# A first batch worked by halves of its heads, w_in begun on half of its depth, and other PSUM banks and more of the squares on GpSimd for the first product

## The chip, the cores and the metric

The kernel runs on one core of one Trainium2 chip. The metric is device time in microseconds (us) of that core; lower is better. Before the change the median was 289.12 us over four runs (288.58 to 289.61), so single runs differ by about 0.3%. All times below that begin with a point on a time axis ("at 31.12") are microseconds from the start of one traced execution; a trace is one execution.

A ratio is the mean time of one kernel's fast runs over the mean of the other's fast runs of the same rounds, so it is not quite the ratio of the medians that are quoted beside it.

## The reference

An attention without a score matrix feeds a layer with a sine-based activation:

```
q_s = softmax(q) over the 64 columns of a head
k_s = softmax(k) over the 576 positions
kv  = k_s^T v                    (64 x 64 per head)
x   = q_s kv                     -> 4608 tokens x 512
h   = x @ w_in                   (512 x 2048)
g   = h + sin(alpha * h)^2 / alpha
out = g @ w_out                  (2048 x 512)
```

There are 8 batches of 576 positions and 8 heads. The tokens are worked in 9 tiles of 512 (t = 0 to 8), so tile 1 needs batch 1 of the attention.

## The kernel before

TensorE (PE) multiplies, ScalarE (ACT) takes exponentials, sines, some squares and copies, VectorE (DVE) normalises and adds, GpSimd (POOL) takes the other squares and issues the loads of w_in, of w_out and of some of v of batch 0, SyncE (SP) issues nearly all the rest. The start loads batch 0 and builds x transposed in four slices `xT[:, 0..3]`, each 128 deep; slices 0 and 1 need one half of the heads (`ii = 0`), slices 2 and 3 the other.

```python
load("q", q, 0, halves=True); load("k", k, 0, halves=True)     # SP's queue, halves of the heads
...
GP_CP(held, staged["q", 0][...])                  # holds POOL's queue until half of q is there
... v in three pieces on POOL's queue ...
for c0, c1 in ((0, 256), (256, 512), (512, 1024), (1024, 1536), (1536, 2048)):
    load_win(c0, c1)                              # two DMAs each, cast to bf16 on the way
...
for ii in range(2):
    kv_mm(0, ii, ps_e, split=True)
    kv_norm(0, ii, ii + 1)
for c in range(4):
    xp = ps_h.tile([128, MF], F32, name="hp", tag="h")
    attn_chunk(0, c, 0, 8, xp)
    (ACT_CP, DVE_CP)[c % 2](xT[:, c, 0:MF], xp)
nc.scalar.activation(zero, zero, AX.Sin)          # loads the sine table
```

The first tile of tokens is then 16 blocks of 128 columns of w_in. Each is four matmuls into a PSUM buffer, a sine, a square on the engine that a letter names (D, P or A), and a sum on DVE, which frees the buffer. Blocks use four buffers of `ps_h` in turn, and two more of `ps_e` where `wide` says so. The product with w_out takes the four `ps_h` buffers for its accumulators.

```python
def mm_h(t, ni, wide=None, k0=0, k1=4):
    ...
    elif wide and ni % 6 in ((2, 3) if t == 0 else (4, 5)):
        hp = wide()
    else:
        hp = ps_h.tile([128, MF], F32, name="hp", tag="h")
...
for ni in range(nN):
    h_slot(0, ni, "DPAPPAPPAPPAPPAP"[ni], lag, lent)
    flush(lag, 1)                                 # sum of block ni - 1
    if ni in late:
        late[ni]()                                # q and k of batch 1, rest of w_out
...
os = o_quad(0, accs, [DVE_CP, ACT_CP, DVE_CP, ACT_CP])   # 64 matmuls with w_out
take(os, 20)
... small attention product: the last 64 positions of batch 0 ...
take(os, 26)
... batch 1: exp, normalise, transpose ...
take(os, 8)
kv_mm(1, 0, ps_e, split=True)                     # needs v of batch 1
```

The softmax here doesn't subtract the row's maximum and nothing guards it: scores larger than these inputs give would overflow.

## Time and profile before

| | before |
|---|---|
| time, median | 289.12 us |
| traced span | 286.8 us |
| PE busy | 274.9 us (96%) |
| first product with w_in | 15.74 us |
| first sine / first square on POOL | 17.73 / 19.06 us |
| small attention product | 34.09 us |
| first cast of v of batch 1 | 41.35 us |
| first product of tile 1 | 47.23 us |

The last rows are starting times in the trace.

```profile
15.74 1.95 PE L234 MATMUL hp<-xT,win 128*128 128x512 bf16 x8
...
41.35 1.17 ACT L131 CAST vb<-st_v 128x1152 bf16<-128x1152 f32 x1 [0.20 <-DMA st_v<-in_v_dram]
...
47.23 2.97 PE L234 MATMUL hp<-xT,win 128*128 128x512 bf16 x13
```

The traced execution took 288.60 us, as little as the fastest of the four timed ones (288.58) and 0.5 us less than their median. A difference between this trace and another one is not yet a difference between two kernels.

### The profile page before, as it was taken

The page shows a single profiled execution, that of the slowest core. Times are in us where ns is not written, and L with a number is a line of the kernel's source. Part 1 is how long each engine was busy: PE and PEld are TensorE (multiplying, and loading weights), DVE is VectorE, ACT ScalarE, POOL GpSimd, SP SyncE. Part 2 cuts the span into 40 slices and gives each one's busy share as a digit, 9 for nine tenths or more (in the row PEclk, how much of TensorE's full clock was granted, in tenths as well). Part 3 has the DMA queues.
Part 4 walks back from the last instruction along what each step waited for, and adds up shares of the span by engine and source line. Part 5 has one row for each costly group of instructions (what it writes and reads, how often), then busy time and mean ns, then how long its engine had stood idle before and what let it go on. Part 6 is the DMA issues. An engine that isn't in the chain of part 4 may idle for free.

```text
span 286.8 us, 4259 instructions
## 1 busy us (share of the span) xinstructions
PE 274.9 (96%) x1570; PEld 130.6 (46%) x1570; DVE 188.5 (66%) x281; ACT 226.6 (79%) x320; POOL 81.6 (28%) x77
## 2 busy tenths in 40 slices
PE   1899999999999999999999999999999999999994
PEld 0444454445454445444544454445444444444443
DVE  3867775899968668756775677757674555555412
ACT  4889756999489999899889988998877777777500
POOL 4859420674766571005300530032000000000000
PEclk9999999999999999999999999999999999999999
DMA  7999999946799957129910990116011111111142
GB/s 253 309 205 242 269 391 408 307 169 191 167 199 402 361 184 120 38 43 358 289 37 21 336 308 27 37 39 139 17 39 37 37 37 39 37 37 38 41 109 73
DMA packets 37381, 45.77 MB, mean 160 GB/s; under 512 B 15968, under 2 KB 20848, under 8 KB 37360
## 3 DMA queue, kind: packets, MB, share of 16 engines
q1 hardware_dynamic: 32032, 39.98, 46.3%
q0 software_dynamic: 5136, 5.38, 10.2%
q8 instruction: 12, 0.20, 0.3%
q10 hardware_dynamic: 192, 0.14, 0.2%
q14 instruction: 9, 0.07, 0.1%
HBM read 36.71 MB, written 9.44 MB: 161 GB/s over the span
## 4 chain that ended last, share of the span: by engine, by line
PE 84%; DMA 7%; DVE 5%; POOL 1%; ACT 1%; issue 1%; SPq 0%; POOLq 0%
PE hp L234 38%; PE op L254 35%; DMA st_v<-in_v_dram 4%; PE hh L234 3%; PE kvp L157 2%; PE xp L206 2%; DMA qT<-qn 2%; DMA st_q<-in_q_dram 1%; DVE qs L144 1%; PE op L532 1%; PE op L234 1%; ACT s L240 1%; DVE qn L146 1%; POOL qn L146 1%; POOL s L244 1%
## 5 line engine op out<-in xcount | busy, mean ns | idle before, releaser
L250 DVE SCALAR_TENSOR_TENSOR g<-s,inva_sb,hp 128x512 bf16<-128x512 f32 x130 | 96.1, 745 | 64.1 <-ACT s L242 54.2
L234 PE MATMUL hp<-xT,win 128*128 128x512 bf16 x520 | 129.7, 379 | 0.0
L254 PE MATMUL op<-wout,g 128*128 128x512 bf16 x496 | 124.2, 379 | 0.0
L240 ACT ACTIVATE s<-hp,alpha_sb 128x512 f32<-128x512 f32 x130 | 87.6, 682 | 25.4 <-PE hp L234 24.3
L234 PEld LDWEIGHTS <-win 128*128 128x128 bf16 x576 | 56.3, 98 | 67.4 <-issue 0.4
L254 PEld LDWEIGHTS <-g 128*128 128x128 bf16 x560 | 54.1, 98 | 61.7 <-issue 0.9
L242 ACT ACTIVATE s<-s 128x512 f32<-128x512 f32 x112 | 70.5, 630 | 3.5
L146 POOL TENSOR_TENSOR qn<-qe,qs 128x1152 bf16<-128x1152 bf16 x12 | 25.3, 2128 | 73.2 <-DVE qs L140 63.1
L244 POOL TENSOR_TENSOR s<-s 128x512 f32<-128x512 f32 x29 | 30.5, 1061 | 24.8 <-ACT s L240 24.3
L260 DVE COPY o<-op 128x512 f32<-128x512 f32 (+2 forms) x33 | 22.1, 669 | 9.6 <-PE op L254 7.1
L117 ACT ACTIVATE ke<-st_k 128x1152 bf16<-128x1152 f32 x16 | 17.9, 1151 | 4.8 <-DMA st_k<-in_k_dram 4.1
L117 ACT ACTIVATE qe<-st_q 128x1152 bf16<-128x1152 f32 x16 | 17.9, 1156 | 2.8 <-DMA st_q<-in_q_dram 2.8
L139 DVE TENSOR_REDUCE qs<-qe 128x36 f32<-128x2304 bf16 x5 | 12.8, 2553 | 8.7 <-ACT qe L117 8.6
L131 POOL CAST vb<-st_v 128x1152 bf16<-128x1152 f32 x12 | 13.6, 1162 | 10.4 <-DMA st_v<-in_v_dram 10.4
L254 PE MATMUL hp<-wout,g 128*128 128x512 bf16 x64 | 15.1, 379 | 0.0
L209 DVE CAST xT<-xp 128x512 bf16<-128x512 f32 (+1 forms) x18 | 13.4, 742 | 0.0
L117 ACT ACT_TABLE_LOAD x7 | 9.0, 1283 | 1.3 <-PEq L546 1.2
L157 PEld LDWEIGHTS <-ke 64*128 64x128 bf16 x288 | 8.2, 93 | 3.5 <-ACT s L242 1.3
L157 PE MATMUL kvp<-vb,ke 64*128 64x130 bf16 x288 | 9.7, 216 | 0.0
L234 PE MATMUL hh<-xT,win 128*128 128x512 bf16 x40 | 9.4, 379 | 0.0
L144 DVE TENSOR_REDUCE qs<-qe 128x18 f32<-128x1152 bf16 x6 | 8.0, 1329 | 2.1 <-ACT qe L117 2.1
L206 PE MATMUL xp<-qT,kbd 128*128 128x256 bf16 (+1 forms) x40 | 8.2, 286 | 0.4 <-DVE xT L209 0.3
(68 smaller groups left out, 117.9 us busy)
## 6 DMA issues: line engine op xcount, KB each, us to landing
out_dram<-o SPq DMA_DIRECT2D x70, 128.0 KB, 2.3
st_q<-in_q_dram SPq DMA_DIRECT2D x6, 1152.0 KB, 6.3
st_k<-in_k_dram SPq DMA_DIRECT2D x6, 1152.0 KB, 8.2
st_v<-in_v_dram SPq DMA_DIRECT2D x6, 1152.0 KB, 10.3
st_q<-in_q_dram SPq DMA_DIRECT2D x4, 576.0 KB, 5.5
st_k<-in_k_dram SPq DMA_DIRECT2D x4, 576.0 KB, 7.1
wout<-in_moe_w_out_dram POOLq DMA_DIRECT2D x4, 512.0 KB, 11.2
win<-in_moe_w_in_dram POOLq DMA_DIRECT2D x6, 256.0 KB, 7.1
```

The costliest lines, as they stand in the source:

```text
L117: nc.scalar.activation(dst[:, :, ii * 128:(ii + 1) * 128].rearrange("p j (x d) -> p x j d", x=2), src[:, ii::2], AX.Exp)
L131: engs[ii](vv[:, 2 * ii:2 * ii + 2, :, 0:D], staged["v", b][:, ii::2])
L146: engs[ii % len(engs)].tensor_tensor(qn[:, ii].rearrange("p j (x d) -> p j x d", x=2), qe[:, ii], part.unsqueeze(3).to_broadcast([128, J, ...
L157: nc.tensor.matmul(kvp[:, e, ii * 130:(ii + 1) * 130], ke[r, j, ii * 128:(ii + 1) * 128], vt[r, j, ii * 130:(ii + 1) * 130], start=(j == 0 ...
L206: nc.tensor.matmul(xp[:, e, 0:n], kt[:, e, ii], qT[:, ii, j0:j1, e * 64:(e + 1) * 64], start=True, stop=True)
L234: nc.tensor.matmul(hp, win[:, ki, ni * 128:(ni + 1) * 128], xT[:, ki, t * MF:(t + 1) * MF], start=(ki == 0), stop=(ki == 3))
L240: nc.scalar.activation(s, hp, AX.Sin, scale=alpha_sb[:, ni:ni + 1])
L242: nc.scalar.activation(s, s, AX.Square)
L244: nc.gpsimd.tensor_tensor(s, s, s, op=ALU.mult)
L250: nc.vector.scalar_tensor_tensor(G[t][:, ni], in0=s, scalar=inva_sb[:, ni:ni + 1], in1=hp, op0=ALU.mult, op1=ALU.add)
L254: nc.tensor.matmul(acc, G[t][:, ni, j * 128:(j + 1) * 128], wout[:, ni, :], start=(ni == 0), stop=(ni == nN - 1))
L260: eng(o[:, cols], acc)
```

## The change

The intent is that PE starts on w_in earlier. Batch 0 is worked by halves: q, k and v of the first half of the heads are loaded and used before k and v of the second half. When slices 0 and 1 of xT are there, four blocks of w_in do their first slices, while the other half is still worked on. These four blocks need four `ps_h` buffers, so the extra buffers of `ps_e` go to blocks 4, 5, 9, 10, 14, 15. The row of squares gives POOL 12 in place of 10. Two transposes of q move from the start into the w_out product.

```diff
-    for c0, c1 in ((0, 256), (256, 512), (512, 1024), (1024, 1536), (1536, 2048)):
-        load_win(c0, c1)
+    GP_CP(singles.tile([128, 1], F32, name="held"), staged["k", 0][:, 0, 0, 0:1])
+    load0(GP, "v", v, 1, 0, 5)
+    load0(GP, "v", v, 1, 5, 9)
+    load_win(0, 512, slice(0, 2))
+    load_win(0, 512, slice(2, 4))
+    for c0 in (512, 1024, 1536):
+        load_win(c0, c0 + 512)
 ... cut: exp, cast, transposes and kv of the first half, warm-up matmuls ...
+    nc.scalar.activation(zero, zero, AX.Sin)
+    xp = [ps_h.tile([128, MF], F32, name="hp", tag="h") for _ in range(2)]
+    for c in range(2):
+        attn_chunk(0, c, 0, 8, xp[c])
+    DVE_CP(xT[:, 0, 0:MF], xp[0])
+    ACT_CP(A["qT", 0][:, 1, 0:8], tp1)
+    ACT_CP(xT[:, 1, 0:MF], xp[1])
+    kv_mm(0, 1, ps_e, split=True)
+    kv_norm(0, 1, 2)
+    for ni in range(4):
+        mm_h(0, ni, None, 0, 1)
+    xp = ps_e.tile([128, 2, MF], F32, name="xp", tag="a")
+    for e in range(2):
+        attn_chunk(0, 2 + e, 0, 8, xp[:, e])
+    for e in range(2):
+        (DVE_CP, ACT_CP)[e](xT[:, 2 + e, 0:MF], xp[:, e])
+    for ni in range(4):
+        mm_h(0, ni, None, 1, 2)
 ... cut ...
-        elif wide and ni % 6 in ((2, 3) if t == 0 else (4, 5)):
+        elif wide and (ni in (4, 5, 9, 10, 14, 15) if t == 0 else ni % 6 in (4, 5)):
 ... cut ...
-            h_slot(0, ni, "DPAPPAPPAPPAPPAP"[ni], lag, lent)
+            h_slot(0, ni, "DPPPAPPPAPPPAPPP"[ni], lag, lent)
 ... cut ...
-        take(os, 20)
+        take(os, 10)
+        tp = ps_e.tile([128, 2, 128], BF16, name="tp", tag="a")
+        for ii in range(2):
+            q_transpose_ii(0, ii, 8, 9, tp[:, ii:ii + 1])
+        ACT_CP(A["qT", 0][:, :, 8], tp)
+        take(os, 10)
```

More of the change, by code (lines that the diff above doesn't have):

```diff
@@ L102, in load_batch, with load_win @@
         load("v", v, b)
-    def load_win(c0, c1):
+    def load_win(c0, c1, ks=slice(0, 4)):
         n = slice(c0, c1)
         for x in range(2):
-            nc.gpsimd.dma_start(out=win[64 * x:64 * x + 64, :, n], in_=win_v[x][:, :, n])
+            nc.gpsimd.dma_start(out=win[64 * x:64 * x + 64, ks, n], in_=win_v[x][:, ks, n])
     def load_wout(c):
@@ L113, with exp_to @@
     A = {}
-    def exp_to(dst, src):
-        for ii in range(2):
+    def exp_to(dst, src, iis=range(2)):
+        for ii in iis:
             nc.scalar.activation(dst[:, :, ii * 128:(ii + 1) * 128].rearrange("p j (x d) -> p x j d", x=2),
@@ L122, in exp_q, with exp_half @@
         exp_to(A["qe", b], staged["q", b])
+    def exp_half(name, b, ii):
+        if ii == 0:
+            A[name + "e", b] = att2.tile([128, J, 4 * D], BF16, name=name + "e")
+        exp_to(A[name + "e", b], staged[name, b], (ii,))
     def exp_k(b):
@@ L268, with load0 @@
     V, GP = nc.vector, nc.gpsimd
-    load("q", q, 0, halves=True)
-    load("k", k, 0, halves=True)
+    for n in "qkv":
+        staged[n, 0] = stage.tile([128, 4, J, D], F32, name=f"st_{n}", tag="st")
+    def load0(eng, n, t, ii, j0=0, j1=J):
+        eng.dma_start(out=staged[n, 0][:, ii::2, j0:j1].rearrange("p i j d -> p i (j d)"),
+                      in_=src_view(t, 0)[:, ii::2, j0 * D:j1 * D])
+    for n, t, ii in (("q", q, 0), ("k", k, 0), ("q", q, 1), ("v", v, 0), ("k", k, 1)):
+        load0(nc.sync, n, t, ii)
     nc.scalar.dma_start(out=alpha_rows, in_=moe_alpha.rearrange("(no ni) -> no ni", ni=128))
@@ L282 @@
     ps_e = ES.enter_context(tc.tile_pool(name="ps_e", bufs=2, space=PSUM, reuse_waits="tile"))
-    tps = [ps_h.tile([128, 8, 128], BF16, name="tp", tag="h") for _ in range(3)]
+    tp0 = ps_h.tile([128, 8, 128], BF16, name="tp", tag="h")
     warm = ps_h.tile([128, 4, 128], F32, name="warm", tag="h")
@@ L289, with cast_v0 @@
     nc.vector.reciprocal(inva_sb, alpha_sb)
-    GP_CP(singles.tile([128, 1], F32, name="held"), staged["q", 0][:, 0, 0, 0:1])
-    staged["v", 0] = st = stage.tile([128, 4, J, D], F32, name="st_v", tag="st")
-    for ii, j0, j1 in ((0, 0, 9), (1, 0, 5), (1, 5, 9)):
-        GP.dma_start(out=st[:, ii::2, j0:j1].rearrange("p i j d -> p i (j d)"),
-                     in_=src_view(v, 0)[:, ii::2, j0 * D:j1 * D])
-    for c0, c1 in ((0, 256), (256, 512), (512, 1024), (1024, 1536), (1536, 2048)):
-        load_win(c0, c1)
+    def cast_v0(ii, j0, j1, eng):
+        vv = vb[0].rearrange("p j (i c) -> p i j c", i=4)
+        eng(vv[:, 2 * ii:2 * ii + 2, j0:j1, 0:D], staged["v", 0][:, ii::2, j0:j1])
+    GP_CP(singles.tile([128, 1], F32, name="held"), staged["k", 0][:, 0, 0, 0:1])
[5 more added lines that the diff above has]
+        load_win(c0, c0 + 512)
     for c in range(2):
         load_wout(c)
-    exp_q(0)
-    exp_k(0)
     def warm_up(n):
@@ L308, in warm_up @@
             nc.tensor.matmul(warm, identb, A["qe", 0][:, 0:4, 0:128], start=True, stop=True)
-    def cast_v0(ii, j0, j1, eng):
-        vv = vb[0].rearrange("p j (i c) -> p i j c", i=4)
-        eng(vv[:, 2 * ii:2 * ii + 2, j0:j1, 0:D], staged["v", 0][:, ii::2, j0:j1])
+    exp_half("q", 0, 0)
+    exp_half("k", 0, 0)
+    exp_half("q", 0, 1)
     warm_up(7)
@@ L317 @@
     q_tile(0)
-    q_transpose_ii(0, 0, 0, 8, tps[0])
-    ACT_CP(A["qT", 0][:, 0, 0:8], tps[0])
-    cast_v0(0, 0, 5, ACT_CP)
-    cast_v0(0, 5, 9, DVE_CP)
-    warm_up(6)
-    q_transpose_ii(0, 1, 0, 8, tps[1])
-    for ii in range(2):
-        q_transpose_ii(0, ii, 8, 9, tps[2][:, ii:ii + 1])
-    cast_v0(1, 0, 5, DVE_CP)
-    cast_v0(1, 5, 9, ACT_CP)
-    ACT_CP(A["qT", 0][:, 1, 0:8], tps[1])
-    ACT_CP(A["qT", 0][:, :, 8], tps[2][:, 0:2])
-    for ii in range(2):
-        kv_mm(0, ii, ps_e, split=True)
-        kv_norm(0, ii, ii + 1)
-    for c in range(4):
-        xp = ps_h.tile([128, MF], F32, name="hp", tag="h")
-        attn_chunk(0, c, 0, 8, xp)
-        (ACT_CP, DVE_CP)[c % 2](xT[:, c, 0:MF], xp)
-    nc.scalar.activation(zero, zero, AX.Sin)
+    q_transpose_ii(0, 0, 0, 8, tp0)
+    cast_v0(0, 0, 9, ACT_CP)
+    ACT_CP(A["qT", 0][:, 0, 0:8], tp0)
+    exp_half("k", 0, 1)
+    warm_up(2)
+    kv_mm(0, 0, ps_e, split=True)
+    warm_up(3)
+    kv_norm(0, 0, 1)
+    tp1 = ps_e.tile([128, 8, 128], BF16, name="tp", tag="a")
+    q_transpose_ii(0, 1, 0, 8, tp1)
+    cast_v0(1, 0, 5, DVE_CP)
+    cast_v0(1, 5, 9, DVE_CP)
+    nc.scalar.activation(zero, zero, AX.Sin)
+    xp = [ps_h.tile([128, MF], F32, name="hp", tag="h") for _ in range(2)]
[15 more added lines that the diff above has]
+        mm_h(0, ni, None, 1, 2)
     def h_slot(t, ni, sq, lag, wide=None):
-        hp = mm_h(t, ni, wide, 2 if t < 2 and ni < 2 else 0)
+        hp = mm_h(t, ni, wide, 2 if ni < (4, 2, 0)[min(t, 2)] else 0)
         lag.append((t, ni, hp, sine(t, ni, hp, sq)))
@@ L373 @@
                 10: lambda: load_wout(3), 13: lambda: load("k", k, 1, halves=True, gate=DVE_CP)}
-        for ki in range(2):
-            for ni in range(2):
-                mm_h(0, ni, lent, ki, ki + 1)
         for ni in range(nN):
-            h_slot(0, ni, "DPAPPAPPAPPAPPAP"[ni], lag, lent)
+            h_slot(0, ni, "DPPPAPPPAPPPAPPP"[ni], lag, lent)
             flush(lag, 1)
```

## The prediction

> **What bounds the kernel now.** I read the page first, then PE by stages, then the chain of waits, then each engine's timeline from 0 to 47 us.
>
> ```profile
> span 286.8 us, 4259 instructions
> ...
> PE 274.9 (96%) x1570; PEld 130.6 (46%) x1570; DVE 188.5 (66%) x281; ACT 226.6 (79%) x320; POOL 81.6 (28%) x77
> ...
> DMA  7999999946799957129910990116011111111142
> ```
>
> PE is busy for 274.9 of 286.8 us. The DMA engines are full in the first eight slices but the first (7.2 us each). PE busy by stages (length, PE busy and count, clock, DMA share, GB/s):
>
> ```profile
> 0.00:15.90 15.90, 8.26 (x73) 1.00 0.97 273
> 15.90:29.60 13.70, 13.70 (x64) 1.00 1.21 236
> 29.60:46.10 16.50, 16.38 (x122) 1.00 1.10 341
> ```
>
> PE idles 7.64 us before the first product with w_in and 0.12 us in the next 30 us. So a PE start that is earlier or later by d moves everything behind it by d, unless a transfer or another engine is late too. The chain of waits (start, us, what) shows that one transfer is:
>
> ```profile
> 32.24 10.53 DMA st_v<-in_v_dram
> ...
> 42.79 0.76 DVE vb L131
> ```
>
> The second half of v of batch 1 lands at 42.77 us and PE wants it at 43.80. The first half landed near 41.33, its cast ended at 42.52, and PE used it at 42.64. The DMA engines have moved data without a gap from 2.8 us to there, so these two dates are set by bytes, and the change takes no bytes away. **An earlier PE can thus win some 0.1 us before it waits for v; a later PE loses in full.** The last view is the start, ACT, POOL and PE from the timeline:
>
> ```profile
> 16.32 1.28 ACT L337 ACT_TABLE_LOAD   x1
> 17.62 0.20 ACT L337 ACTIVATE zero<-zero 128x1 f32<-128x1 f32 x1
> 17.73 1.25 ACT L240 ACTIVATE s<-hp,alpha_sb 128x512 f32<-128x512 f32 x2
> ...
> 19.06 1.04 POOL L244 TENSOR_TENSOR s<-s 128x512 f32<-128x512 f32 x1 [2.70 <-ACT s L240]
> ...
> 25.24 0.80 POOL L110 DMA_DIRECT2D wout<-in_moe_w_out_dram  x1
> ...
> 28.02 0.79 POOL L110 DMA_DIRECT2D wout<-in_moe_w_out_dram  x1
> 28.83 3.17 POOL L244 TENSOR_TENSOR s<-s 128x512 f32<-128x512 f32 x3
> ...
> 29.61 4.64 PE L254 MATMUL hp<-wout,g 128*128 128x512 bf16 x20
> 34.09 0.28 PE L214 MATMUL xp<-qT,kbd 128*128 128x64 bf16 x4
> ...
> 42.64 0.68 PE L157 MATMUL kvp<-vb,ke 64*128 64x130 bf16 x18
> ```
>
> The first sine starts at 17.73, behind the table load; POOL's first square at 19.06, its tenth and last ends at 32.0. PE starts the second product (w_out) at 29.61 without a wait.
>
> **What the Trainium skill says.** "ScalarE: Activation LUTs", section "What ACT_TABLE_LOAD costs", gives about 1283 ns for a load; the trace has 1.28 us. "GPSIMD Engine Reference", section "4.1 Engine selection", says that a two-input elementwise operation is about twice as slow there as on VectorE; the trace has 1.04 us on POOL against 0.69 on DVE and 0.63 on ACT for the same square, so 1.5 to 1.7 times. "DMA: Bandwidth & Descriptors", section "Issuing engines are not separate DMA queues", has all queues share one set of engines; the trace agrees: in each microsecond from 29 to 36 both queues move data and together they fill the engines. "TensorE: Matmul & The Clock Gate", section "What's actually happening", has the clock halved until PE has been busy about 3.4 us; the seven warm-up products take 3.02 us (431 ns each) where later ones take 216 ns apart. They stay, so I expect the same clock.
>
> **The start, part by part.** I lay the new order, as built, end to end with durations of the old trace. *Loads:* a half of q, k or v lands each 1.45 us from 4.92: q0 4.92, k0 6.4, q1 7.85, v0 9.25, k1 about 10.9 (two small slices share with the GpSimd queue), v1 in two pieces about 12.0 and 12.6, the first half of the 512 columns of w_in about 14.0.
> *ACT:* exp of q0 to 6.1, of k0 to 7.6, of q1 to 9.0; cast of v0 9.25 to 10.4 (1.17); copy of qT 0.95, to 11.4; exp of k1 1.17, to 12.6; table load and dummy 1.4, to 14.0; second qT copy 0.92, to 14.9; xT block 1, 0.58, to 15.5.
> *DVE:* unchanged to the end of the second normalisation at 12.15; kv norm 0.8, to 12.9; two casts of v1 0.82, to 13.75; xT block 0, 0.68, to 14.4; second kv norm 0.8, to 15.2.
> *PE:* block 0 of xT allows the first product with w_in at 14.45, against 15.74. Four blocks on one input slice: three at 0.216 us each go at once, but the fourth takes the PSUM buffer that xT block 1 is copied from, until 15.5. Behind it two attention products, four second slices, then slices 3 and 4 of block 0: 15.55 + 7 x 0.216 to the last start, + 0.38 to its end = **17.4 to 17.7 us for the first complete block**. (It is about 16.75 before, but its sine waits for the table until 17.73.) So the first sine starts at the same 17.7 as before. PE has by then done more: 64 products that ended their issue at 29.6 end it at 15.55 + 0.216 x (1 + 2 + 60) = 29.15. The gain at PE is **0.45 us** by 29 us.
>
> **The squares and banks.** POOL has 12 squares in place of 10, ACT 3 in place of 5. ACT gains 2 x 0.63 us but has room: four sines and a square take about 3.0 us, four blocks of PE 3.45. POOL does not: 12 x 1.03 + 2 issues of w_out x 0.8 = 14.0 us. First square: sines 1 and 2 end at 18.95, so POOL runs without a break from 19.0 to 33.0 (32.0 before). Three waits follow.
> (a) Squares 1, 2, 3 fall in a row, so DVE's sum of block 4, behind that of block 3, ends at about 23.5; block 9 takes its bank and PE wants it at 23.1: **0.45 us**, which uses up the gain.
> (b) The four accumulators of the w_out product take the buffers of blocks 8, 11, 12, 13. Block 11's square is POOL's ninth: 19.0 + 9 x 1.03 + 1.6 = 29.85, its sum 0.75, to 30.6. The second matmul of the product needs it; PE gets there at 29.85 with (a), and stood there at 29.83 before without a wait. **+0.8 us.** In the old order block 11 was squared by ACT.
> (c) After 10 matmuls (2.16 us, at 32.6) come the two transposes that moved here. They take the bank of block 14, whose square is the eleventh: 31.9, sum to 32.95. **+0.35 us**, and 0.15 for the transposes.
> PE reaches the small attention product at 30.45 + 2.16 + 0.4 + 0.15 + 2.16 = 35.3, against 34.09: **+1.2 us**. From there the order is the old one. At 41 us the transposes of batch 1 need qn, for which exp of q starts some 2.5 us later (behind the new qT copy); I get DVE done at about 41.4 and PE's second group at 41.7, so no more loss. Later v is no longer waited for, which takes back the 0.1 us. PE has next to no idle time behind (0.5 us from 46 to 280), so the lateness stays to the end: 289.1 + 1.1 = **290.2 us**.
>
> **The rivals.**
> 1. *The start gain comes through.* If the fourth block or the table load didn't hold, block 0 of hp is bounded by the second kv norm at 15.2, and would be complete at 17.15; then everything above is 0.5 us less. Even with POOL free, PE would be 0.5 to 1 us early at 29 us and wait for v at 42.5. For it: the intent of the change, and the earlier PE start at 14.45. Against it: the DMA engines without a gap. Result 288.6 to 289.2.
> 2. *POOL is the bound* (my choice): 289.8 to 290.6.
> 3. *A late load at the start.* w_in's first pieces are issued some 0.7 us later, behind k0, and need only 5.2 us to landing where the fastest took 5.9 before; if they take 5.9, the first product begins at 14.8, which the fourth block hides. If k1, fifth in its queue and sharing, lands after 11.4, ACT's row moves by that: first sine 18.2, result 290.7 to 291.3.
> 4. *The clock drops*, since there are 5 warm-ups in place of 6 after the first seven, and more gaps. PE's gaps are all under 1 us from 9.2 to 15.6, so I give it little: each matmul of a slow 3.4 us would cost 0.2 more, up to 1.7 us.
>
> **Range and chances.** The rivals span 288.6 to 291.3, so 80% for 288.6 to 291.4 with 290.2 in the middle. The whole lead before the first product is 15.9 us, of which the change can touch some 1.3; 2% is 5.8 us. Faster by over 2%: 0.01; within 2%: 0.97; slower by over 2%: 0.02.
>
> **What would show it.** Right: first product with w_in near 14.5, broken at its fourth matmul until about 15.5; first sine near 17.7; POOL busy without a gap from 19 to 33; PE idle about 1 us at its second w_out matmul, waiting for DVE's sum behind POOL, and again before the two transposes; small attention product near 35.3. Wrong: POOL with gaps between its squares, PE at the small attention product before 34.1, or a PE wait for v's cast near 42.5. If first sines start before 17, (a) to (c) shrink by as much, and rival 1 holds.

## The result

The changed kernel took 289.63 us (289.57 to 289.73, four runs) against 289.12, a ratio of 1.0018 (95% interval 1.0000 to 1.0037). Timed again in the first experiment it was 0.53 us behind. By the means of the same rounds it was 0.5 us behind in the first timing and 1.0 us (ratio 1.0036) in the second, where two of the six runs lie 0.9 and 1.7 us above their median. It is the same within 2%, and it is slower by half a microsecond to one: the earlier start won nothing.

The profile's page of the changed kernel (busy time of PE and the other engines, and the DMA engines' busy tenths in 40 slices):

```profile
span 287.8 us, 4228 instructions
...
PE 273.8 (95%) x1541; PEld 130.3 (45%) x1569; DVE 188.5 (66%) x281; ACT 225.6 (78%) x317; POOL 82.6 (29%) x78
...
DMA  7999999855899958119900990115111111111142
```

The same bound as before: PE, and DMA engines that are full for the first 50 us. (The page lists 29 fewer matmuls than before while the weight loads differ by one: some matmul records are missing from this trace, so PE's busy sum is about as before and isn't used to compare.) The timeline of ACT, POOL, DVE, PE and PE's weight loads (PEld), lines of the changed kernel numbered five later than before (L239 is L234, L259 is L254, L249 is L244); in brackets the idle time before the instruction and what ended it:

```profile
14.89 0.56 PEld L239 LDWEIGHTS <-win 128*128 128x128 bf16 x4 [1.22 <-DMA win<-in_moe_w_in_dram]
...
17.14 0.58 ACT L361 CAST xT<-xp 128x512 bf16<-128x512 f32 x1 [2.19 <-DVE xT L361]
...
18.19 2.42 ACT L245 ACTIVATE s<-hp,alpha_sb 128x512 f32<-128x512 f32 x4 [0.47 <-PE hp L239]
...
19.54 6.14 POOL L249 TENSOR_TENSOR s<-s 128x512 f32<-128x512 f32 x6 [1.59 <-ACT s L245]
...
29.23 4.03 POOL L249 TENSOR_TENSOR s<-s 128x512 f32<-128x512 f32 x4
30.32 1.41 DVE L255 SCALAR_TENSOR_TENSOR g<-s,inva_sb,hp 128x512 bf16<-128x512 f32 x2 [1.05 <-POOL s L249]
31.12 2.10 PE L259 MATMUL hp<-wout,g 128*128 128x512 bf16 x9 [0.56 <-DVE g L255]
...
35.48 0.28 PE L219 MATMUL xp<-qT,kbd 128*128 128x64 bf16 x4
...
42.63 1.17 ACT L136 CAST vb<-st_v 128x1152 bf16<-128x1152 f32 x1 [0.27 <-DMA st_v<-in_v_dram]
...
44.06 0.76 DVE L136 CAST vb<-st_v 128x1152 bf16<-128x1152 f32 x1 [0.72 <-DMA st_v<-in_v_dram]
```

Line by line: PE's first weights of w_in came at 14.89, when their load had landed. ACT's copy of the fourth slice of xT waited for DVE's copy of the third. The first sine therefore started at 18.19, later than before (17.73), although PE had begun earlier. POOL worked its 12 squares and two issues from 19.54 to 33.26 without a gap. DVE's sum of block 11 waited for POOL, and PE waited for that sum before its second matmul with w_out. The small attention product came 1.39 us later than before. The casts of the two halves of v of batch 1 began when their loads had landed, 1.28 and 1.27 us later than before.

The chain of waits of the changed kernel (start, duration, what; steps of at most 0.04 us left out) runs through POOL there:

```profile
22.65 3.04 POOL s L249 x3
25.69 0.74 POOL wout L110
26.45 2.04 POOL s L249 x2
28.49 0.73 POOL wout L110
29.23 1.06 POOL s L249
30.32 0.76 DVE g L255
31.12 2.10 PE hp L259 x9
```

A table of the milestones (starting times, one trace each), with the experiments that the text uses:

| | before | changed | changed, again | squares_only | split_xp | old_row | tp_early |
|---|---|---|---|---|---|---|---|
| first exp (q has landed) | 4.94 | 4.56 | 4.59 | 4.89 | 4.69 | 4.79 | 4.62 |
| first product with w_in | 15.74 | 14.92 | 14.95 | 15.90 | 14.72 | 14.68 | 14.25 |
| first sine | 17.73 | 18.19 | 18.22 | 17.89 | 17.51 | 18.15 | 17.40 |
| first square on POOL | 19.06 | 19.54 | 19.57 | 19.23 | 18.86 | 19.50 | 18.75 |
| small attention product | 34.09 | 35.48 | 35.41 | 35.05 | 34.78 | 35.10 | 33.80 |
| first cast of v, batch 1 | 41.35 | 42.63 | 41.64 | 41.52 | 42.01 | 42.66 | 41.45 |
| cast of v's second half | 42.79 | 44.06 | 43.19 | 42.93 | 43.42 | 44.06 | 42.89 |
| first product of tile 1 | 47.23 | 48.50 | 48.24 | 47.87 | 47.87 | 48.50 | 47.33 |
| span | 286.8 | 287.8 | 287.4 | 287.5 | 287.2 | 287.9 | 286.8 |

The first row is a warning: the first load lands up to 0.4 us earlier in one execution than in another, whatever the kernel (4.62 in win_half_only, which is the kernel before but for the pieces of w_in, and 4.94 in the kernel before). A difference of up to 0.4 us in the rows below it can be that alone. The traces of the changed kernel had the early load. Against win_half_only, which had it too (its small attention product at 33.80), the changed kernel is not 1.3 to 1.4 but 1.6 to 1.7 us late there.

The cast of v's second half and the first product of tile 1 belong together. Where that cast waited for its load, tile 1 starts 4.44 or 4.45 us after it, in all nine such traces with the order of work unchanged there: before, changed, split_xp, old_row, tp_early, split_oldrow (45.39 and 49.83), split_oldrow_win (43.49 and 47.93), win_half_only (43.43 and 47.87) and v_on_sp (46.33 and 50.77). In the four where v had landed before DVE came to it, the distance is 4.94 to 5.06 us (changed again, squares_only, no_wout3, win_cols). So v's landing set the start of tile 1 in the kernel before already, and in the first trace of the changed kernel as well, where v's cast and tile 1 are late by the same 1.27 us. In the second trace, and in squares_only, PE came last.

### The profile page after: what moved, and what is told of

Its sections match the earlier page's. It is cut to its first block, busy times and chain, and to the rows that moved or that the text cites. A ratio compares the mean times of both kernels' runs of the same rounds, so it can differ in the third digit from the quotient of the medians.

```text
span 287.8 us, 4228 instructions
## 1 busy us (share of the span) xinstructions
PE 273.8 (95%) x1541; PEld 130.3 (45%) x1569; DVE 188.5 (66%) x281; ACT 225.6 (78%) x317; POOL 82.6 (29%) x78
## 3 DMA queue, kind: packets, MB, share of 16 engines
q0 software_dynamic: 4480, 4.79, 9.7%
## 4 chain that ended last, share of the span: by engine, by line
PE 87%; DVE 4%; POOL 3%; ACT 2%; issue 1%; DMA 1%
PE op L259 37%; PE hp L239 36%; PE hp L259 5%; PE kvp L162 3%; POOL s L249 2%; PE xp L211 2%; PE hh L239 2%; DMA st_q<-in_q_dram 1%; PE op L560 1%; PE op L239 1%; ACT s L245 1%; DVE qn L151 1%; DVE qs L149 1%; PE xp L219 1%; DVE g L255 1%
## 5 line engine op out<-in xcount | busy, mean ns | idle before, releaser
L239 PE MATMUL hp<-xT,win 128*128 128x512 bf16 x512 | 129.5, 379 | 1.8 <-DVE kbd L175 1.1
L259 PE MATMUL op<-wout,g 128*128 128x512 bf16 x479 | 121.8, 379 | 1.1 <-issue 0.5
L239 PEld LDWEIGHTS <-win 128*128 128x128 bf16 x576 | 56.0, 98 | 69.5 <-issue 2.1
L259 PEld LDWEIGHTS <-g 128*128 128x128 bf16 x560 | 54.1, 98 | 61.8 <-issue 1.3
L247 ACT ACTIVATE s<-s 128x512 f32<-128x512 f32 x110 | 69.3, 630 | 3.5
L249 POOL TENSOR_TENSOR s<-s 128x512 f32<-128x512 f32 x31 | 32.4, 1059 | 21.9 <-ACT s L245 21.5
L259 PE MATMUL hp<-wout,g 128*128 128x512 bf16 x62 | 15.0, 379 | 0.8 <-DVE g L255 0.6
L239 PE MATMUL hh<-xT,win 128*128 128x512 bf16 x39 | 9.5, 378 | 0.2
```

The source lines that it names most:

```text
L239: nc.tensor.matmul(hp, win[:, ki, ni * 128:(ni + 1) * 128], xT[:, ki, t * MF:(t + 1) * MF], start=(ki == 0), stop=(ki == 3))
L247: nc.scalar.activation(s, s, AX.Square)
L249: nc.gpsimd.tensor_tensor(s, s, s, op=ALU.mult)
L259: nc.tensor.matmul(acc, G[t][:, ni, j * 128:(j + 1) * 128], wout[:, ni, :], start=(ni == 0), stop=(ni == nN - 1))
```

## The experiments

There were twelve, each timed in five rounds beside the kernel before. My theory was that POOL's row of squares costs PE what the start wins, and more. The rivals were that the start is late by itself, and that v of batch 1, which the DMA engines bring at a date of their own, leaves no room for a gain.

### The changed kernel again (after_again)

No edit.

> The changed kernel once more, beside the others on the same chip. The trace has it 1.0 to 1.1 us behind the kernel before from 75 us on; the first timing had 0.5 us between the medians. Expected: 0.4 to 1.1 us slower than before, so a ratio of 1.0015 to 1.004. If it were equal or faster here, the lateness in the trace would not be the kernel's own.

Measured: 289.41 us against 288.88, ratio 1.0036 (1.0016 to 1.0056), which is 0.5 us by medians and 1.0 us by means. The lateness is the kernel's own. Its six runs reach from 289.21 to 291.08, a wider spread than the first timing had. The trace names the load of w_in, for 0.85 us, as what PE's first product waited for.

### The old row of squares on the changed kernel (old_row)

```diff
-            h_slot(0, ni, "DPPPAPPPAPPPAPPP"[ni], lag, lent)
+            h_slot(0, ni, "DPAPPAPPAPPAPPAP"[ni], lag, lent)
```

> The changed kernel with the squares of the first block of tokens handed out as before (10 for POOL, 5 for ACT, 1 for DVE). Theory 'POOL is the bound': POOL ends about 2 us earlier, PE no longer idles 0.56 us at its second matmul with w_out nor at blocks 9 to 11, the small attention product starts near 34.7 us in place of 35.5, and the whole is 0.4 to 0.8 us faster than the changed kernel. Rival 'the late first sine is the cause' (18.19 us in place of 17.73, because of w_in's landing and the second xT copy): nothing moves after the start, same time within 0.2 us.

PE's timeline in this run:

```profile
24.19 1.89 PE L239 MATMUL hh<-xT,win 128*128 128x512 bf16 x8 [0.46 <-DVE g L255]
...
30.25 2.32 PE L259 MATMUL hp<-wout,g 128*128 128x512 bf16 x10
32.84 0.27 PE L191 MATMUL tp<-identb,qn 128*128 128x128 bf16 x2 [0.27 <-DVE g L255]
...
35.10 0.28 PE L219 MATMUL xp<-qT,kbd 128*128 128x64 bf16 x4
...
43.88 0.69 PE L162 MATMUL kvp<-vb,ke 64*128 64x130 bf16 x18 [0.16 <-ACT vb L136]
```

and a line of DVE's:

```profile
44.06 0.76 DVE L136 CAST vb<-st_v 128x1152 bf16<-128x1152 f32 x1 [1.10 <-DMA st_v<-in_v_dram]
```

The ten w_out matmuls run through without the wait at the second, as the theory said, and the small attention product is 0.3 to 0.4 us earlier than in the two traces of the changed kernel (I had expected 0.8). It is not more because the old row doesn't fit the new banks. Block 9 takes the bank of block 4, whose square is now POOL's, and PE waits for its sum: block 9 starts 0.63 us after PE was free for it, where the second trace of the changed kernel has 0.47, and the transposes 0.43 us in place of 0.16. These two take back 0.4 of the 0.72 us. The same wait of 0.46 us at block 9 is in split_oldrow_win, tp_early and more_before_v.

The time was 289.71 us, ratio 1.0034 (1.0018 to 1.0050): no gain. The first k-v product of batch 1, at 43.88, still came 0.16 us before that of the changed kernel's first trace; tile 1 starts at 48.50 in both, 4.44 us behind the cast of v's second half, which started at 44.06 in both. So POOL's row is a bound, but not the only one: taking it away alone gives nothing back.

### The last attention products of the start in two tiles (split_xp)

```diff
-    xp = ps_e.tile([128, 2, MF], F32, name="xp", tag="a")
+    xp = [ps_e.tile([128, 2, MF], F32, name="xp", tag="a")[:, 0] for _ in range(2)]
     for e in range(2):
-        attn_chunk(0, 2 + e, 0, 8, xp[:, e])
+        attn_chunk(0, 2 + e, 0, 8, xp[e])
     for e in range(2):
-        (DVE_CP, ACT_CP)[e](xT[:, 2 + e, 0:MF], xp[:, e])
+        (DVE_CP, ACT_CP)[e](xT[:, 2 + e, 0:MF], xp[e])
```

> The changed kernel with the last two attention products of the start in two tiles in place of one, so that ACT's copy of the fourth block of xT need not wait for DVE's copy of the third (17.11 us in the trace, where the products were done near 16.4). Theory: that copy starts 0.6 to 0.7 us earlier, the first complete block is done 0.3 to 0.5 us earlier, POOL starts its first square 0.3 to 0.5 us earlier and PE's second w_out matmul, which hangs on POOL, moves by as much: 0.3 to 0.5 us faster than the changed kernel. Rival 'the start doesn't set the end, the row of POOL or v's landing does': the first sine is earlier but the time is the same within 0.15 us.

ACT's and POOL's timeline in this run:

```profile
16.21 0.59 ACT L361 CAST xT<-xp 128x512 bf16<-128x512 f32 x1 [1.16 <-PE xp L219]
17.51 2.42 ACT L245 ACTIVATE s<-hp,alpha_sb 128x512 f32<-128x512 f32 x4 [0.71 <-PE hp L239]
...
18.86 6.12 POOL L249 TENSOR_TENSOR s<-s 128x512 f32<-128x512 f32 x6 [1.82 <-ACT s L245]
```

ACT's copy now waits for PE alone and starts at 16.21 in place of 17.14. Sine, POOL and PE's second w_out matmul (30.41) all came 0.7 us earlier, and the small attention product 0.6 to 0.7. The trace is plain, though it is the fastest of the five runs (289.02). The time isn't: 289.72 us as median, but a ratio of 1.0022 (1.0009 to 1.0035) where the changed kernel beside it had 1.0036. The medians say no gain and the means say 0.4 us; it stays unclear.

### The new squares and banks on the kernel before (squares_only)

```diff
-        elif wide and ni % 6 in ((2, 3) if t == 0 else (4, 5)):
+        elif wide and (ni in (4, 5, 9, 10, 14, 15) if t == 0 else ni % 6 in (4, 5)):
...
-            h_slot(0, ni, "DPAPPAPPAPPAPPAP"[ni], lag, lent)
+            h_slot(0, ni, "DPPPAPPPAPPPAPPP"[ni], lag, lent)
```

> The kernel before with only the new row of squares and the new banks, start unchanged. Theory 'POOL is the bound': first square at 19.06 as before, POOL busy to about 33.0 (12 squares and two issues), block 11's sum at about 30.6, so PE idles 0.6 to 1.0 us at its second w_out matmul and everything behind is that much late: 0.5 to 1.0 us slower than before. Rival 'only the start matters': same as before within 0.2 us.

PE's timeline in this run:

```profile
30.01 0.38 PE L254 MATMUL hp<-wout,g 128*128 128x512 bf16 x1
30.95 4.26 PE L254 MATMUL hp<-wout,g 128*128 128x512 bf16 x19 [0.56 <-DVE g L250]
35.05 0.28 PE L214 MATMUL xp<-qT,kbd 128*128 128x64 bf16 x4
```

With the old start, the wait before the second w_out matmul appears, of the same size as in the changed kernel, and the time is 289.51 us against 288.88, ratio 1.0020 (1.0008 to 1.0032). This part alone costs 0.6 us, where the whole change beside it cost 0.5 by medians and 1.0 by means. The edit changes the banks too; that the wait is the row's is shown by old_row, where it is gone with the new banks in place. That settles the sign of the theory.

### Both repairs together (split_oldrow)

The edits of old_row and split_xp on one kernel:

```diff
-            h_slot(0, ni, "DPPPAPPPAPPPAPPP"[ni], lag, lent)
+            h_slot(0, ni, "DPAPPAPPAPPAPPAP"[ni], lag, lent)
...
-    xp = ps_e.tile([128, 2, MF], F32, name="xp", tag="a")
+    xp = [ps_e.tile([128, 2, MF], F32, name="xp", tag="a")[:, 0] for _ in range(2)]
```

> Both removals at once on the changed kernel: two tiles for the last attention products of the start, and the old row of squares. Each alone moved PE at the small attention product (35.4 us in the changed kernel, 34.1 before): to 34.8 and to 35.1. Together about 34.4, and no idle PE at the second w_out matmul. Theory 'two bounds side by side, POOL and then v of batch 1': PE then waits for the cast of v at 42.6 to 44 us, as it began to with the old row alone (0.16 us there, and late kv norms), so only a part comes through: 288.8 to 289.3, still not faster than before. Rival 'only POOL and the late start': all of it comes through, 0.9 us faster than the changed kernel and as fast as before, without a wait for v.

Measured: 289.70 us against 289.20, ratio 1.0018 (0.9996 to 1.0039), and six runs from 288.95 to 290.87. The traced one, of span 289.1, is the slowest, and its loads were late from the start: the exponential of the second half of q began at 8.17, against 7.52 in the changed kernel. PE's timeline shows what it met:

```profile
19.71 1.89 PE L239 MATMUL hh<-xT,win 128*128 128x512 bf16 x8 [0.60 <-DMA win<-in_moe_w_in_dram]
...
44.03 1.46 PE L259 MATMUL hp<-wout,g 128*128 128x512 bf16 x6 [1.02 <-DMA wout<-in_moe_w_out_dram]
```

PE waited for w_in at block 4 and for w_out before v. These aren't the waits that I had named. Tile 1 started at 49.83, again 4.44 us behind the cast of v's second half (45.39). With POOL out of the way PE met the loads in this execution; in split_oldrow_win it met v's, and w_in's for 0.2 us.

### One megabyte less to load (no_wout3)

Its output is wrong, which doesn't matter for the time.

```diff
+    nc.vector.memset(wout[:, 12:16, :], 0.0)
...
-                10: lambda: load_wout(3), 13: lambda: load("k", k, 1, halves=True, gate=DVE_CP)}
+                13: lambda: load("k", k, 1, halves=True, gate=DVE_CP)}
```

> The kernel split_oldrow without the load of the last quarter of w_out (zeros are set there at the start), so 1 MB less is read before v of batch 1; its result is wrong on purpose. Theory 'v's landing is a bound of its own': v lands 1.5 to 2.6 us earlier, near 40 to 41 us, PE doesn't wait for its cast, and the time falls by 0.3 to 0.8 us below split_oldrow. Rival 'the bytes don't matter': v lands earlier but PE's row stays as it is, same time as split_oldrow within 0.15 us.

The first cast of v started at 40.20, and PE met no wait for v or w_out, though in the traced run it still waited 1.1 us for w_in. The time was 288.74 us, ratio 0.9983 (0.9961 to 1.0006), beside 1.0018 for split_oldrow in the same rounds. That is 0.35% or 1.0 us of the means for a quarter of w_out, somewhat more than expected. The two intervals just overlap, and POOL also has one issue less, so this speaks for the loads as a bound of their own without proving how much of it is v. In its trace v's second half no longer held anything: tile 1 started 5.06 us behind its cast.

### w_in by columns, as before (win_cols)

```diff
-    load_win(0, 512, slice(0, 2))
-    load_win(0, 512, slice(2, 4))
+    load_win(0, 256)
+    load_win(256, 512)
```

> The changed kernel with the first 512 columns of w_in loaded as before, by 256 columns with the whole depth, in place of by half the depth. In the traces the GpSimd queue writes 0.14 to 0.18 MB/us from 12 to 16 us with the half-depth pieces and 0.18 to 0.20 with the old ones. Theory 'the piece shape slows the queue': 0.18 to 0.20 MB/us again, the first pieces land about 14.0 to 14.4 in place of 14.9; PE's first product starts at 14.2 to 14.5 but its third waits for the second 256 columns until about 15.3, so the first sine is within 0.2 us of the changed kernel's 18.2 and the time too. Rival 'the queue is slow because it begins later, with fewer transfers in flight': still 0.14 to 0.18 MB/us.

The traces say what the GpSimd queue wrote from 12 to 16 us: 0.78 MB in the kernel before, 0.64 and 0.67 in the changed kernel's two traces, 0.78 here. The pieces have the same bytes (128 KB written), as 256 rows of 512 bytes in one case and 128 rows of 1024 bytes in the other. All fourteen traces together say less than these four. From 12 to 13 us the queue wrote 0.18 to 0.20 MB in the seven with the first shape and 0.09 to 0.15 in the seven with the second; from 13 to 16 us it is 0.40 to 0.60 and 0.43 to 0.61, which overlap. So the shape goes with a difference of 0.03 to 0.11 MB in one microsecond near the start of these pieces, and a lasting one isn't shown. The time, 289.97 us against 289.20 and a ratio of 1.0025 (1.0005 to 1.0044), didn't improve. In the traced run the second half of q landed more than a microsecond late (its exponential started at 8.84, against 7.52 in the changed kernel), so its milestones can't be compared.

### Both repairs and w_in by columns (split_oldrow_win)

split_oldrow with the edit of win_cols:

```diff
-    load_win(0, 512, slice(0, 2))
-    load_win(0, 512, slice(2, 4))
+    load_win(0, 256)
+    load_win(256, 512)
```

> split_oldrow with w_in's first 512 columns by 256 columns, as before. If the piece shape slows the queue, v of batch 1 lands 0.4 to 0.9 us earlier than in split_oldrow and the time falls by 0.2 to 0.5 us, to that of the kernel before or 0.2 us below it. If not, same as split_oldrow within 0.15 us.

Measured: 289.31 us against 289.20, ratio 1.0008 (0.9981 to 1.0034). From 12 to 16 us the queue wrote 0.73 MB, and v's first cast started at 42.08. Here tile 1 started 4.44 us behind the cast of v's second half (43.49). It is as fast as the kernel before within what can be told. The gain over split_oldrow lies within the intervals.

### Only the half-depth pieces on the kernel before (win_half_only)

The kernel before with the changed kernel's loads of w_in:

```diff
-    for c0, c1 in ((0, 256), (256, 512), (512, 1024), (1024, 1536), (1536, 2048)):
-        load_win(c0, c1)
+    load_win(0, 512, slice(0, 2))
+    load_win(0, 512, slice(2, 4))
+    for c0, c1 in ((512, 1024), (1024, 1536), (1536, 2048)):
+        load_win(c0, c1)
```

> The kernel before with one thing of the change: the first 512 columns of w_in in pieces of half the depth. Theory 'these pieces slow the GpSimd queue': 0.14 to 0.18 MB/us from 12 to 16 us in place of 0.18 to 0.20; the first product of the first block waits for its second pair of pieces at about 15.5 us, and v of batch 1 lands 0.4 to 1.0 us later than the 41.3 of before, with PE waiting for it, as it has no slack there: 0.3 to 0.8 us slower than before. Rival 'in the old order the queue has slack': same time within 0.2 us.

PE's timeline in this run:

```profile
33.80 0.28 PE L214 MATMUL xp<-qT,kbd 128*128 128x64 bf16 x4
...
43.26 0.69 PE L157 MATMUL kvp<-vb,ke 64*128 64x130 bf16 x18 [0.84 <-ACT vb L131]
```

PE was 0.3 us earlier than in the trace of before at the small attention product, since its first load had landed 0.3 us earlier (first exp at 4.62), and then waited 0.84 us for the cast of v, which began at 42.04 in place of 41.35. This wait is as much v's lateness as PE's earliness, so by itself it doesn't show that the kernel before has no room to start earlier; the trace of before does, with tile 1 already 4.44 us behind the cast of v's second half. The queue wrote 0.69 MB from 12 to 16 us. The time was 289.08 us against 288.98, ratio 1.0007 (0.9990 to 1.0025): these pieces alone have no cost that these runs can show, against my expectation of 0.3 to 0.8 us.

### The two transposes back in the start (tp_early)

split_oldrow_win with this:

```diff
-    tp1 = ps_e.tile([128, 8, 128], BF16, name="tp", tag="a")
+    tp1 = ps_e.tile([128, 16, 128], BF16, name="tp", tag="a")
     q_transpose_ii(0, 1, 0, 8, tp1)
+    for ii in range(2):
+        q_transpose_ii(0, ii, 8, 9, tp1[:, 8 + ii:9 + ii])
...
-        take(os, 10)
-        ... transposes into a ps_e tile, copy ...
-        take(os, 10)
+        take(os, 20)
```

> split_oldrow_win with the two last transposes of q back in the start, in the tile of the other eight, in place of after the tenth w_out matmul, where they cost 0.27 us and a wait of 0.26 for block 14's sum. Expected: PE at the small attention product 0.4 to 0.5 us earlier (34.5), 0.2 to 0.5 us faster than split_oldrow_win if v's landing (42.1 us there) lets it through, and nothing if PE waits for v's cast then.

PE's timeline in this run:

```profile
33.80 0.28 PE L219 MATMUL xp<-qT,kbd 128*128 128x64 bf16 x4
...
42.67 0.69 PE L162 MATMUL kvp<-vb,ke 64*128 64x130 bf16 x18 [0.25 <-ACT vb L136]
```

With these losses repaired, but for the wait at block 9 (0.46 us, at 23.43), PE came to the small attention product 0.3 us before the kernel before, as its first load had landed 0.3 us before: level, no more (win_half_only, with the same early load and the old start, is at 33.80 too). Then it waited for v, and its span is that of the kernel before, 286.8; like that one, it is the fastest of its runs (288.54). The time was 289.33 against 288.98, ratio 1.0017 (0.9997 to 1.0037).

### v on SP's queue (v_on_sp)

The second half of v of batch 0 goes behind k on SP's queue, and POOL's queue waits for the second half of q, so that w_in comes first on it. On tp_early:

```diff
-    for n, t, ii in (("q", q, 0), ("k", k, 0), ("q", q, 1), ("v", v, 0), ("k", k, 1)):
+    for n, t, ii in (("q", q, 0), ("k", k, 0), ("q", q, 1), ("v", v, 0), ("k", k, 1), ("v", v, 1)):
...
-    GP_CP(singles.tile([128, 1], F32, name="held"), staged["k", 0][:, 0, 0, 0:1])
-    load0(GP, "v", v, 1, 0, 5)
-    load0(GP, "v", v, 1, 5, 9)
+    GP_CP(singles.tile([128, 1], F32, name="held"), staged["q", 0][:, 1, 0, 0:1])
```

> tp_early with the second half of v of batch 0 on SP's queue behind k, and the GpSimd queue held until the second half of q has landed, so that w_in is the first thing on it. Expected: v0's second half lands near 12, the first w_in pieces near 13.3 to 14, so PE's first product hangs on xT alone; 0 to 0.4 us faster than tp_early, and 0.2 to 0.6 us faster than before if all of it comes through. If v of batch 1 bounds, equal to before within 0.2 us.

A miss: 290.21 us, ratio 1.0046 (1.0022 to 1.0070). PE's first product started on time (14.43) and its third matmul waited 1.8 us for the second 256 columns of w_in, which landed near 16.8. POOL began to issue w_in at 8.91, against 7.87 in the changed kernel. The traced run is the slowest of the six (291.86).

### More work ahead of v (more_before_v)

```diff
-        take(os, 8)
+        take(os, 10)
         kv_mm(1, 0, ps_e, split=True)
```

on tp_early.

> tp_early with two more w_out matmuls (0.43 us of work that needs no v) ahead of the first k-v product of batch 1, where PE waited 0.25 us for v's cast. Theory 'v's landing is what holds the repaired kernel': the wait before that product is gone or below 0.1 us, the work behind v is 0.43 us shorter, and the time falls by 0.2 to 0.4 us against tp_early: 0 to 0.3 us faster than before. Rival 'something else holds it' (the chain of norm and copies behind v, or the queue's spread): the wait moves behind v, same time as tp_early within 0.15 us, no faster than before.

The wait before the first k-v product is gone from the trace, and tile 1 starts 4.00 us behind the cast of v's second half (43.45 and 47.45) in place of 4.44: the two matmuls moved ahead of v are worth their 0.43 us there. The time was 288.82 us against 289.00, ratio 0.9992 (0.9969 to 1.0015). It has the lowest median of all correct versions, and it can't be told from the kernel before. Against tp_early (1.0017, on another chip) the intervals overlap, so the expected gain isn't shown in time.

## Why the prediction was right, and where it was not

The range held (289.63 in 288.6 to 291.4), and the sign and the wait behind POOL's row were right. The size was up to twice too large: 1.1 us forecast, 0.5 by the medians of both timings, 0.5 and 1.0 by their means. By its own steps:

**The first product with w_in, 14.45: near, for another reason.** It started at 14.92, held by w_in's landing, the third rival. The break that I put at the fourth matmul, until 15.5, didn't come: the four matmuls ran on from 14.92, and the copy that the fourth needs was done at 14.96. The attention products behind them started at 15.78, where I had them at 15.77. That the dates agree is luck: two errors cancel. ACT's copy came 0.5 us before its forecast date, about 0.4 of it because the first load landed early in this execution (4.56 against 4.92), and w_in landed at 14.89 where I had about 14.0. Nor was the late w_in hidden, as that rival had it: copy and k-v norms were done by 14.96, so the attention products could have started near 15.2 (an estimate from these dates and the 0.216 us of a matmul) in place of 15.78.

**The first complete block at 17.4 to 17.7, and the first sine at 17.7: failed by 0.5.** The working laid the copies of the third and fourth slices of xT side by side on DVE and ACT. They read two halves of one tile, and in this program ACT waited for DVE. I passed over it. split_xp removes it, and the first sine moves from 18.19 to 17.51.

**The squares: right.** 19.0 to 33.0 forecast, 19.54 to 33.26 measured without a gap; 13.7 us for what I put at 14.0. squares_only shows that this part alone makes PE wait and costs about 0.6 us.

**The waits**, counted from when PE was free by its 0.216 us per matmul. (a) at block 9: 0.45 forecast; 0.47 in the second trace of the changed kernel (0.31 of it counted as idle by the view), 0.17 in the first, where PE had lost 0.30 at block 4. (b) at the second w_out matmul: 0.8 forecast; it started at 31.12 where 30.40 (0.216 after the first) was free, so 0.72, of which the view counts 0.56 as idle. (c) at the transposes: 0.35 forecast, 0.16 in both traces, since PE came 0.6 us later than I had it and the block was nearly ready. The sum at the small attention product still came out, at 35.48 and 35.41 against 35.3, but with luck: the late sine took the place of what (c) lacked, and the working was laid on a first load at 4.92 where these executions had it near 4.6.

**"The lateness stays to the end": the term that was mis-sized.** Over the trace of before, the second trace of the changed kernel is late by 1.01 us at the first product of tile 1, by 0.70 at the k-v product near 84 us (83.69 against 82.99) and by 0.6 at the end. So 0.4 us came back after 48 us, where I had carried over all of it. In the first trace it is 1.27, 1.09 and 1.0, near the forecast. Which wait gave it back I didn't test. The base was off as well: the working was laid on an execution of 288.60 us, and its 1.1 us were added to the median of 289.1. Added to that execution's own time they give 289.7, and 289.63 was measured.

**"These two dates are set by bytes": right that v binds, wrong on where, and the date moves.** An earlier PE gains nothing there: no version that repaired PE's losses beat the kernel before beyond doubt, and PE waited 0.84 us for v in win_half_only and 0.25 in tp_early. But the bound sits behind the second half of v, where I saw a margin of its cast's end (43.55) to 43.80: DVE does the k-v norm of the first half only after that cast, and PE waited for this norm before tile 1 (in the trace of before the cast starts at 42.79, the norm ends at 44.86, and the attention product that needs it starts at 44.92). A version with the norm ahead of the cast wasn't run. And the date isn't fixed. With the same bytes the second half's cast, where it waited for its load, started anywhere from 42.79 to 46.33. The share of the half-depth pieces in that isn't shown: 43.42 to 45.39 with them, 42.79 to 46.33 without.

**The rivals.** Rival 1 (the gain comes through, 288.6 to 289.2) was wrong for the changed kernel, and of the repaired ones only the median of more_before_v (288.82) lies there; its limit, v, is the one they met. Rival 3 was right in w_in's late landing and wrong in its being hidden; its first sine of 18.2 came for another reason (k1 did not hold ACT). Rival 4 is not seen: the matmuls with w_in follow each other at 0.216 us from 14.92 on. (The granted clock of 1.00 in the first 46 us of both traces doesn't decide it, as it is 1.00 too in the stage with the warm-up products of 431 ns.)

Three slips of the working had no effect: the first complete block ends eight steps, not seven, after 15.55 (17.66, inside the stated 17.4 to 17.7); before, it is the sixth matmul and so complete at 17.2, not 16.75; and from 33 to 34 us only the GpSimd queue moved data, not both.

What stays open: how the half to one microsecond divides between PE's lateness (POOL's row, the late sine, w_in) and v's landing, which moves by more than that from one execution to the next, and what moves it. The runs of one kernel spread over 1 to 2 us in the later rounds, and differences of 0.3 us can't be told in five rounds.

## What to carry to other kernels

When the bottleneck engine is to start earlier, ask first which other engine and which transfer would have to be earlier too; here POOL's row of squares was within some tenths of binding, the landing of the next batch's v was binding already, and moving PE alone bought nothing. Before moving work to an engine with a low average share, lay its instructions end to end over the stretch concerned: POOL was 29% busy over the span, and 100% over the 14 us that mattered. Give two engines that copy at the same time two tiles, not two halves of one.

## What the Trainium skill lacked or had wrong

- "DMA: Bandwidth & Descriptors", section "Measured (HBM→SBUF, 128 partitions, SWDGE, issued from GpSimd)", gives the rate by size, without the shape of a piece. Here pieces of the same size differed by shape at first: from 12 to 13 us the queue wrote 0.18 to 0.20 MB with pieces of 256 rows of 512 bytes (seven traces), and 0.09 to 0.15 MB with 128 rows of 1024 bytes (seven traces). From 13 to 16 us the two overlap (0.40 to 0.60 and 0.43 to 0.61).
- "ScalarE: Activation LUTs", section "What ACT_TABLE_LOAD costs", adds a drain of about 1380 ns to the load. In the changed kernel the exponential ended at 12.05, the load took 12.07 to 13.35 and the next activation started at 13.36: 1.31 us from one to the other, and no drain.
- None of the pages that I used says that copies by two engines out of two halves of one PSUM tile can come to run one behind the other, as ACT's behind DVE's here. It cost 0.7 us at the first sine (18.19 against 17.51 with two tiles).
